# QKV in blocks of 512, 512, 512 and 384 columns, with transposed x, the weights and silu's halves at other residues of 256 bytes

## The chip, the core and the metric

The kernel runs on one core of a Trainium2 chip. The metric is device time in microseconds (us) of one execution; lower is better. A profile is taken of one further execution. TensorE (PE in the profile) multiplies, VectorE is DVE, ScalarE is ACT, GpSimd is POOL and SyncE is SP; PEld are TensorE's weight loads.

## What is computed

The reference normalises each of 2048 rows of x (640 columns), runs local attention over the result (32 heads of 20, each position looks at 8 positions in steps of 2 backwards), and gates the attention's output with a feed-forward part:

```python
xn = _layernorm(x, axis=-1)
s = _A_ref(xn, A_wqkv, A_wo)          # q, k, v = xn @ wqkv; scores; softmax; values; @ wo
g = _silu(_B_ref(xn, B_w1, B_w2))     # silu(silu(xn @ w1) @ w2)
return x + s * g
```

wqkv is 640 x 1920, wo 640 x 640, w1 640 x 1536, w2 1536 x 640, all float32.

## The kernel before, in words

**Precision.** TensorE is fed `float32r` operands. Every operand is split in a high part, which is its rounded copy, and a low part, which is the rest: `TH`/`TL` for transposed x (and later transposed attention output), `SH`/`SL` for silu(x W1), and the two halves of a slot of the weight ring `WR`. A product is three matmuls: high x high, low x high, high x low. So each logical matmul is issued three times, each with its own load of a 128x128 stationary tile and its own stream of up to 512 columns.

**Tiling.** The 2048 rows are four groups of 512 rows (`groups`), each of four tiles (`T`) of 128 rows. D = 640 is five chunks (`DC`) of 128, F = 1536 twelve (`FC`).

**Stages of a group**, in TensorE's order. `qkv_phase`: four blocks (`NQ`) of eight heads; for each block, five chunks c, four tiles t, three matmuls (L622 to L624): the stationary operand is a 128x128 piece of transposed x, the moving operand 480 columns of wqkv, which are 160 of q, 160 of k and 160 of v, into one PSUM bank for each t. ScalarE then evacuates k and v (L430) and q (L433), DMAs shift some rows of k and v (`halo`), and VectorE does scores and values (L467 to L509) with much delay, into `O`. In group 0 the first block is written out by hand (`first_quarter`, matmuls on L569) so that it can start before all weights have come: it works tile by tile, in passes over the chunks. `wo_phase` for the group before (L656 and L658 with TH/TL as stationary operand): it needs `O` transposed, which `o_chunk` does in five pieces (L419) at fixed places in the QKV stage (`O_AT`), or, for the last group, in the feed-forward stage (`OL_AT`). `ffn_phase`: for each of twelve chunks f, fifteen matmuls of 512 columns (L773 to L775; weights stationary, transposed x moving), silu twice on ScalarE (L779, L780) into `SH[f % 2]` and a float32 copy, the low part on VectorE (L781), and, one chunk later, 24 matmuls with silu's halves as the stationary operand and w2 as the moving one, 384 columns (L656) and 256 columns (L658) in turn. `wo_last` ends the program.

**Weights.** A ring of seven slots of 2 x 640 columns holds the next units (`units`, `w_load`, `w_next`, `w_done`). On first use a unit's raw float32 columns come in by DMA on SP's queue (`raw_load`, L338), are split by ScalarE (L361) and VectorE or GpSimd (L364), and both halves are stored to DRAM (L370); later uses load both halves by one DMA of GpSimd's queue (L353). High half first, low half directly behind it: for a QKV unit at 480 columns = 1920 bytes, for the others at 640 columns = 2560 bytes.

**Order.** TensorE's order is the program's. The other engines' order is made by a planner (`Weave`): every operation has a duration by a cost formula (`mm`, `ac`, `dv`, `po`; 0.45 us for issuing a DMA), a priority and the tiles that it reads and writes, and the planner simulates the program and emits it in order of the simulated start. The queues then run in that order.

**Memory.** All tiles come from one pool, one after the other in the order of the `sb.tile` lines (L194 to L220). `TH` and `TL` are 10240 bytes a tile, a ring slot 5120, silu halves 2048, all multiples of 256 in one partition; `mask` is 128 bytes, the statistics `ST` 48 each, of which a tile takes 64. Before, `st1` stands between `sh1`, `sl1` and `sh0`, `sl0`.

Of the kernel before, what the change touches and what calls it, by code (L numbers as in the profile page):

```python
# [8 lines left out]
F32 = mybir.dt.float32  # L9
F32R = mybir.dt.float32r  # L10
AF = mybir.ActivationFunctionType
# [3 lines left out]
P = 128  # L15
S, D, F, H, DH = 2048, 640, 1536, 32, 20
W = 8
DC, FC = D // P, F // P
NQ = 4
HQ = H // NQ  # L20
CQ = HQ * DH
J = 8
T = 4
TOK = T * P
HALO = W - 1
SCALE = DH ** -0.5
# [22 lines left out]
def tsl(t):  # L49
    return slice(t * P, (t + 1) * P)  # L50
# [120 lines left out]
def local_attention_silu_ffn(ctx: ExitStack, tc: tile.TileContext, x, wqkv, wo, w1, w2, out):  # L171
    nc = tc.nc
    pool = lambda name, bufs, **kw: ctx.enter_context(tc.tile_pool(name=name, bufs=bufs, **kw))
    sb = pool("sb", 1)
# [16 lines left out]
    def tiles(name, n, shape, dtype=F32):  # L191
        return [sb.tile(shape, dtype, name=f"{name}{i}") for i in range(n)]
# [4 lines left out]
    ST = [sb.tile([P, 2, 6], F32, name="st0")]  # L197
    TH = tiles("th", 2, [P, DC, TOK], F32R)
    TL = tiles("tl", 2, [P, DC, TOK], F32R)
    WR = tiles("w", RING, [P, 2 * D], F32R)  # L200
    SH = [None, sb.tile([P, TOK], F32R, name="sh1")]
    SL = [None, sb.tile([P, TOK], F32R, name="sl1")]
    ST.append(sb.tile([P, 2, 6], F32, name="st1"))
    SH[0] = sb.tile([P, TOK], F32R, name="sh0")
    SL[0] = sb.tile([P, TOK], F32R, name="sl0")
    SD = sb.tile([P, 2, T], F32, name="sd")
    mask = sb.tile([P, T, W], F32, name="mask")
    M = tiles("m", 2, [P, T, HQ])
    Z = tiles("z", 2, [P, 2, T, HQ])
    KV = tiles("kv", NQ, [P, 2, HALO + T, CQ])  # L210
    Q = tiles("q", NQ, [P, T, CQ])
    O = sb.tile([P, T, D], F32, name="o")
    PR = sb.tile([P, 2, W, CQ], F32, name="pr")
    L = tiles("l", 2, [P, T, W, HQ])
    E = tiles("e", 2, [P, T, W, HQ])
# [8 lines left out]
    PRK = [("pr", k) for k in range(DC)]  # L224
# [16 lines left out]
    mm = lambda n: n / 2400 + 0.0155  # L241
# [57 lines left out]
    for u in units:  # L299
        n = seen[u] = seen.get(u, 0) + 1  # L300
# [4 lines left out]
    raws = {}  # L305

    def width(u):
        return 3 * CQ if u[0] == "q" else D

    def raw_load(k):  # L310


        if k >= len(fresh):
            return
        i = fresh[k]
        u = units[i]
        n = width(u)
        if k < DC:
            r, kr = PR.rearrange("p t w m -> p (t w m)")[:, k * n:(k + 1) * n], [PRK[k]]
        elif k < early:  # L320
            s = (k - DC) % 6
            r, kr = (RAW[s], [("raw", s)]) if s < 2 else (G[:, s - 2, :], [("g", s - 2, 0), ("g", s - 2, CA)])
            r = r[:, :n]
        else:
            s = k % 2
            r, kr = RAW[s][:, :n], [("raw", s)]
        raws[i] = r, kr
        if u[0] == "q":
            _, q, c = u
            src = wqkv[c * P:(c + 1) * P, :].rearrange("p (s m) -> p s m", s=3)[:, :, q * CQ:(q + 1) * CQ]  # L330
            dst = r.rearrange("p (s m) -> p s m", s=3)
        elif u[0] == "w1":
            src = w1.rearrange("(c p) f -> p c f", p=P)[:, :, u[1] * P:(u[1] + 1) * P]
            dst = r.rearrange("p (c f) -> p c f", c=DC)
        else:
            m = wo if u[0] == "wo" else w2
            src, dst = m[u[1] * P:(u[1] + 1) * P, :], r
        dma(lambda: nc.sync.dma_start(dst, src), [], kr, n * P * 4, 1 + k if k < 2 * DC else clock[0] + 5)  # L338
# [87 lines left out]


    def evac_qkv(g, q, t, ps, kp):
        kv, qq = KV[q], Q[q]
        act(2 * CQ, lambda: nc.scalar.activation(  # L430
            kv[:, :, HALO + t, :], ps[:, CQ:3 * CQ].rearrange("p (s m) -> p s m", s=2), AF.Copy),
            [kp], [("kv", q, t)], 0)
        act(CQ, lambda: nc.scalar.activation(qq[:, t, :], ps[:, :CQ], AF.Copy), [kp], [("q", q, t)], 0)  # L433

    def halo(g, q):
        h, par = groups[g]
# [23 lines left out]

    def scores(g, q):
        i = q % 2
        l, e, m, kv, qq = L[i], E[i], M[i], KV[q], Q[q]
        hk = halo_keys(q)
        pr = 100 + 10 * (NQ * g + q)
        for t in range(0, T, 2):
            dve(2560, lambda t=t: nc.vector.tensor_tensor(  # L467
                out=PR, in0=win(qq[:, t:t + 2, :], W, 0), in1=win(kv[:, 0, t:t + 2, :], W, CQ), op=OP.mult),
                hk + [("q", q, t), ("q", q, t + 1)], PRK, pr, lock=True)
# [12 lines left out]
        act(256, lambda: nc.scalar.activation(e, l, AF.Exp, scale=SCALE), kl, [("e", i)], 0.5, "exp")  # L482
# [33 lines left out]
    def first_quarter(i):  # L516

        ps, ws = {}, []
# [41 lines left out]
        def products(t, steps):  # L560

            o, kp = ps[t]
            for k, c in steps:
                x, kx = (TL, "tl") if k == 1 else (TH, "th")
                wh, wl, kh, kl = ws[c]
                w, kw = (wl, kl) if k == 2 else (wh, kh)
                first, last = t not in given, given.get(t, 0) == 3 * DC - 1
                given[t] = given.get(t, 0) + 1
                pe(mm(480), lambda x=x, c=c, w=w, first=first, last=last: nc.tensor.matmul(  # L569
                    o[:, :3 * CQ], x[i][:, c, tsl(t)], w, start=first, stop=last), [(kx, i, c, t), kw], [kp])  # L570

        def passes(*ks):
            return [(k, c) for k in ks for c in range(DC)]
# [14 lines left out]
        for t in range(T):  # L588
            b, kp = bank()
# [18 lines left out]
    def qkv_phase(g, i, io):  # L608
        for q in range(NQ):
            if g == 0 and q == 0:  # L610
                ps = first_quarter(i)
            else:
                ps = [bank() for t in range(T)]
                for c in range(DC):
                    wh, wl, kh, kl = w_next("q", q, c)
                    for t in range(T):
                        o, kp = ps[t]

                        def unit(c=c, t=t, o=o, wh=wh, wl=wl):
                            o = o[:, :3 * CQ]  # L620
                            hi, lo = TH[i][:, c, tsl(t)], TL[i][:, c, tsl(t)]
                            nc.tensor.matmul(o, hi, wh, start=c == 0, stop=False)  # L622
                            nc.tensor.matmul(o, lo, wh, start=False, stop=False)  # L623
                            nc.tensor.matmul(o, hi, wl, start=False, stop=c == DC - 1)  # L624
# [231 lines left out]
```

## Time and profile before

| What | Value |
|---|---|
| median of 3 runs | 643.29 us (643.25 to 643.55) |
| the profiled execution | 643.21 us |
| its span, from the first instruction to the last | 641.4 us |
| granted TensorE clock | 1.000 |
| TensorE busy | 635.5 us, 99% of the span, 3497 matmuls |
| VectorE busy | 536.6 us, 84% |
| DMA | 162.44 MB, mean 253 GB/s |

A row of the groups reads: line, engine, operation, written tile <- read tiles, shapes, count | busy time, mean time of one in ns | idle time of the engine before them and what ended it. A row of the timeline reads: start in us, duration, engine, line, operation, tiles, shapes and count. A row of the waits reads: engine, tile, line <- whom it waited for: us in all, times, the longest. Matmuls are pipelined, and the profile models their ends, so that durations overlap; the distance from start to start is the time that they take. SPq rows are DMAs being issued by SyncE.

### The profile page before, as it was taken

The page shows a single profiled execution, that of the slowest core. Times are in us where ns is not written, and L with a number is a line of the kernel's source. Part 1 is how long each engine was busy: PE and PEld are TensorE (multiplying, and loading weights), DVE is VectorE, ACT ScalarE, POOL GpSimd, SP SyncE. Part 2 cuts the span into 40 slices and gives each one's busy share as a digit, 9 for nine tenths or more (in the row PEclk, how much of TensorE's full clock was granted, in tenths as well). Part 3 has the DMA queues.
Part 4 walks back from the last instruction along what each step waited for, and adds up shares of the span by engine and source line. Part 5 has one row for each costly group of instructions (what it writes and reads, how often), then busy time and mean ns, then how long its engine had stood idle before and what let it go on. Part 6 is the DMA issues. An engine that isn't in the chain of part 4 may idle for free.

```text
span 641.4 us, 9021 instructions
## 1 busy us (share of the span) xinstructions
PE 635.5 (99%) x3497; PEld 574.4 (90%) x3497; DVE 536.6 (84%) x539; ACT 207.1 (32%) x401; POOL 111.0 (17%) x168
## 2 busy tenths in 40 slices
PE   8999999999999999999999999999999999999997
PEld 6888899998889999999888999999988899899997
DVE  6699999999999889999849999998106999999714
ACT  5436453443534022324332112233313222223130
POOL 4500000001000331111211134111111113311100
PEclk9999999999999999999999999999999999999999
DMA  8999999776999997656699989765579997876522
GB/s 266 348 319 338 350 385 360 278 227 227 306 317 320 294 296 246 193 167 222 174 271 265 298 233 312 245 188 162 173 207 264 274 296 231 281 261 199 170 83 82
DMA packets 64938, 162.44 MB, mean 253 GB/s; under 512 B 5648, under 2 KB 28656, under 8 KB 64896
## 3 DMA queue, kind: packets, MB, share of 16 engines
q0 software_dynamic: 20016, 82.58, 42.5%
q1 hardware_dynamic: 44880, 79.29, 39.1%
q8 instruction: 27, 0.44, 0.3%
q14 instruction: 15, 0.12, 0.1%
HBM read 109.55 MB, written 34.16 MB: 224 GB/s over the span
## 4 chain that ended last, share of the span: by engine, by line
PE 98%; DMA 1%; SPq 1%; ACT 0%; DVE 0%; issue 0%
PE acc L656 22%; PE acc L658 15%; PE acc L623 10%; PE acc L624 10%; PE acc L622 10%; PE rot L775 9%; PE rot L773 9%; PE rot L774 9%; PE rot L419 2%; PE acc L569 2%; DMA pr<-in_A_wqkv_dram 1%; SPq L338 0%; PE rot L745 0%; PE rot L548 0%; SPq L578 0%; ACT w L361 0%
## 5 line engine op out<-in xcount | busy, mean ns | idle before, releaser
L656 PE MATMUL acc<-w,sh 128*128 128x384 f32 x384 | 114.8, 337 | 0.0
L623 PE MATMUL acc<-w,tl 128*128 128x480 f32 x300 | 114.6, 382 | 0.0
L622 PE MATMUL acc<-w,th 128*128 128x480 f32 x300 | 114.5, 382 | 0.0
L624 PE MATMUL acc<-w,th 128*128 128x480 f32 x300 | 113.3, 378 | 0.0
L658 PE MATMUL acc<-w,sh 128*128 128x256 f32 x384 | 107.2, 279 | 0.0
L467 DVE TENSOR_TENSOR pr<-q,kv 128x2560 f32<-128x2560 f32 x32 | 90.3, 2821 | 9.8 <-DMA kv<-kv 9.4
L773 PE MATMUL rot<-th,w 128*128 128x512 f32 x240 | 94.9, 396 | 0.0
L775 PE MATMUL rot<-th,w 128*128 128x512 f32 x240 | 93.7, 391 | 0.0
L774 PE MATMUL rot<-tl,w 128*128 128x512 f32 x240 | 93.7, 390 | 0.0
L499 DVE TENSOR_TENSOR pr<-e,kv 128x2560 f32<-128x2560 f32 x32 | 90.3, 2820 | 0.7
L470 DVE TENSOR_REDUCE l<-pr 128x128 f32<-128x2560 f32 x32 | 90.0, 2812 | 0.2
L779 ACT ACTIVATE sh<-rot 128x512 fp32r<-128x512 f32 x48 | 28.8, 599 | 160.3 <-PE rot L775 160.1
L504 DVE TENSOR_TENSOR pr<-pr 128x1280 f32<-128x1280 f32 x64 | 76.4, 1193 | 1.1
L658 PEld LDWEIGHTS acc<-w,sh 128*128 128x128 f32 x384 | 72.2, 188 | 1.5
L656 PEld LDWEIGHTS acc<-w,sh 128*128 128x128 f32 x384 | 72.1, 188 | 1.5
L353 POOL DMA_DIRECT2D w<-half_w x72 | 38.4, 533 | 189.0 <-PE acc L658 95.6
L353 POOL DMA_DIRECT2D w<-half_q x52 | 27.8, 534 | 243.5 <-PE rot L775 125.8
L622 PEld LDWEIGHTS acc<-w,th 128*128 128x128 f32 x300 | 56.3, 188 | 9.1
L624 PEld LDWEIGHTS acc<-w,th 128*128 128x128 f32 x300 | 56.3, 188 | 8.2
L623 PEld LDWEIGHTS acc<-w,tl 128*128 128x128 f32 x300 | 56.4, 188 | 7.9
L656 PE MATMUL acc<-w,sl 128*128 128x384 f32 x192 | 58.5, 336 | 0.0
L775 PEld LDWEIGHTS rot<-th,w 128*128 128x128 f32 x240 | 45.0, 188 | 9.7
(88 smaller groups left out, 977.6 us busy)
## 6 DMA issues: line engine op xcount, KB each, us to landing
w<-half_w POOLq DMA_DIRECT2D x72, 640.0 KB, 5.4
w<-half_q POOLq DMA_DIRECT2D x52, 480.0 KB, 4.3
half_w<-w SPq DMA_DIRECT2D x24, 640.0 KB
half_q<-w SPq DMA_DIRECT2D x20, 480.0 KB
w<-half_wo POOLq DMA_DIRECT2D x15, 640.0 KB, 5.3
kv<-kv SPq DMA_DIRECT2D x16, 560.0 KB
kv<-kv SPq DMA_DIRECT2D x16, 420.0 KB
gate<-in_B_w_dram SPq DMA_DIRECT2D x16, 320.0 KB
```

The costliest lines, as they stand in the source:

```text
L467: dve(2560, lambda t=t: nc.vector.tensor_tensor(out=PR, in0=win(qq[:, t:t + 2, :], W, 0), in1=win(kv[:, 0, t:t + 2, :], W, CQ), op=OP.mult ...
L470: dve(2560, lambda t=t: nc.vector.tensor_reduce(out=l[:, t:t + 2].rearrange("p t w h -> p (t w h)"), in_=PR.rearrange("p t w (h d) -> p (t ...
L499: dve(2560, lambda t=t, v=v: nc.vector.tensor_tensor(out=PR.rearrange("p t w (h d) -> p t (w h) d", d=DH), in0=e[:, t:t + 2].rearrange("p ...
L504: dve(2 * n * CQ, lambda n=n: nc.vector.tensor_tensor(out=PR[:, :, 0:n, :], in0=PR[:, :, 0:n, :], in1=PR[:, :, n:2 * n, :], op=OP.add), [] ...
L622: nc.tensor.matmul(o, hi, wh, start=c == 0, stop=False)
L623: nc.tensor.matmul(o, lo, wh, start=False, stop=False)
L624: nc.tensor.matmul(o, hi, wl, start=False, stop=c == DC - 1)
L656: nc.tensor.matmul(a[t][0][:, :CA], st, w[:, :CA], start=first, stop=last)
L658: nc.tensor.matmul(b[t // 2][0][:, h * CB:(h + 1) * CB], st, w[:, CA:], start=first and h == 0, stop=last, skip_group_check=True)
L773: nc.tensor.matmul(h, wh[:, cs], TH[i][:, c, :], start=c == 0, stop=False)
L774: nc.tensor.matmul(h, wh[:, cs], TL[i][:, c, :], start=False, stop=False)
L775: nc.tensor.matmul(h, wl[:, cs], TH[i][:, c, :], start=False, stop=c == DC - 1)
```

## The change

q's columns are cut differently from k's and v's. A block still brings the 160 columns of k and 160 of v of its eight heads, but with them 192 columns of q (`BQ`), so that three blocks have 512 columns and the last, with 64 of q, has 384. `Q` becomes one tile of 640 columns for each t; the scores of block q wait for the evacuations of blocks q - 1 and q. A raw QKV unit is loaded by two DMAs, q apart from k and v, and the planner is told 0.9 us for issuing them. The low half of a QKV unit begins 512 or 384 columns behind the high one, 2048 or 1536 bytes, both multiples of 256.

`mask` moves from behind the silu halves to before the weight ring, and `st1` to behind the ring and before all four silu halves. Modulo 256, `TH` and `TL` then begin at 0 (counted from the first of them), the weights at 128, the silu halves at 192; before, `TH`, `TL`, the weights, `sh1` and `sl1` began at 0 and `sh0` and `sl0` at 64.

```diff
+BQ = 192
...
     TL = tiles("tl", 2, [P, DC, TOK], F32R)
+    mask = sb.tile([P, T, W], F32, name="mask")
     WR = tiles("w", RING, [P, 2 * D], F32R)
-    SH = [None, sb.tile([P, TOK], F32R, name="sh1")]
-    SL = [None, sb.tile([P, TOK], F32R, name="sl1")]
     ST.append(sb.tile([P, 2, 6], F32, name="st1"))
-    SH[0] = sb.tile([P, TOK], F32R, name="sh0")
-    SL[0] = sb.tile([P, TOK], F32R, name="sl0")
+    SH = tiles("sh", 2, [P, TOK], F32R)
+    SL = tiles("sl", 2, [P, TOK], F32R)
     SD = sb.tile([P, 2, T], F32, name="sd")
-    mask = sb.tile([P, T, W], F32, name="mask")
...
-    Q = tiles("q", NQ, [P, T, CQ])
+    Q = sb.tile([P, T, D], F32, name="q")
...
     def width(u):
-        return 3 * CQ if u[0] == "q" else D
+        return qcols(u[1]) + 2 * CQ if u[0] == "q" else D
+
+    def qcols(b):
+        return min(BQ, D - b * BQ)
...
-            src = wqkv[c * P:(c + 1) * P, :].rearrange("p (s m) -> p s m", s=3)[:, :, q * CQ:(q + 1) * CQ]
-            dst = r.rearrange("p (s m) -> p s m", s=3)
+            w = qcols(q)
+            all3 = wqkv[c * P:(c + 1) * P, :].rearrange("p (s m) -> p s m", s=3)
+
+            def go():
+                nc.sync.dma_start(r[:, :w], all3[:, 0, q * BQ:q * BQ + w])
+                nc.sync.dma_start(r[:, w:].rearrange("p (s m) -> p s m", s=2), all3[:, 1:, q * CQ:(q + 1) * CQ])
+            dma(go, [], kr, n * P * 4, 1 + k if k < 2 * DC else clock[0] + 5, dur=0.9)
+            return
...
-        act(CQ, lambda: nc.scalar.activation(qq[:, t, :], ps[:, :CQ], AF.Copy), [kp], [("q", q, t)], 0)
+        act(w, lambda: nc.scalar.activation(Q[:, t, q * BQ:q * BQ + w], ps[:, :w], AF.Copy), [kp], [("q", q, t)], 0)
...
-                hk + [("q", q, t), ("q", q, t + 1)], PRK, pr, lock=True)
+                hk + [("q", b, u) for b in range(max(q - 1, 0), q + 1) for u in (t, t + 1)], PRK, pr, lock=True)
...
-                        pe(3 * mm(480), unit, t_keys(i, [c], [t]) + [kh, kl], [kp])
+                        pe(3 * mm(n), unit, t_keys(i, [c], [t]) + [kh, kl], [kp])
```

More of the change, by code (lines that the diff above doesn't have):

```diff
@@ L428, in evac_qkv @@
     def evac_qkv(g, q, t, ps, kp):
-        kv, qq = KV[q], Q[q]
+        kv, w = KV[q], qcols(q)
         act(2 * CQ, lambda: nc.scalar.activation(
-            kv[:, :, HALO + t, :], ps[:, CQ:3 * CQ].rearrange("p (s m) -> p s m", s=2), AF.Copy),
+            kv[:, :, HALO + t, :], ps[:, w:w + 2 * CQ].rearrange("p (s m) -> p s m", s=2), AF.Copy),
             [kp], [("kv", q, t)], 0)
-        act(CQ, lambda: nc.scalar.activation(qq[:, t, :], ps[:, :CQ], AF.Copy), [kp], [("q", q, t)], 0)
+        act(w, lambda: nc.scalar.activation(Q[:, t, q * BQ:q * BQ + w], ps[:, :w], AF.Copy), [kp], [("q", q, t)], 0)
     def halo(g, q):
@@ L462, in scores @@
         i = q % 2
-        l, e, m, kv, qq = L[i], E[i], M[i], KV[q], Q[q]
+        l, e, m, kv, qq = L[i], E[i], M[i], KV[q], Q[:, :, q * CQ:(q + 1) * CQ]
         hk = halo_keys(q)
@@ L568, in products @@
                 given[t] = given.get(t, 0) + 1
-                pe(mm(480), lambda x=x, c=c, w=w, first=first, last=last: nc.tensor.matmul(
-                    o[:, :3 * CQ], x[i][:, c, tsl(t)], w, start=first, stop=last), [(kx, i, c, t), kw], [kp])
+                pe(mm(512), lambda x=x, c=c, w=w, first=first, last=last: nc.tensor.matmul(
+                    o, x[i][:, c, tsl(t)], w, start=first, stop=last), [(kx, i, c, t), kw], [kp])
         def passes(*ks):
@@ L615, in qkv_phase, with unit @@
                     wh, wl, kh, kl = w_next("q", q, c)
+                    n = width(("q", q, c))
                     for t in range(T):
                         o, kp = ps[t]
-                        def unit(c=c, t=t, o=o, wh=wh, wl=wl):
-                            o = o[:, :3 * CQ]
+                        def unit(c=c, t=t, o=o, wh=wh, wl=wl, n=n):
+                            o = o[:, :n]
                             hi, lo = TH[i][:, c, tsl(t)], TL[i][:, c, tsl(t)]
```

## The prediction

> **What bounds the kernel now.** I read the page first, then the waits and the chain, then the timeline of TensorE stretch by stretch. The page gives the frame: the span, the busy row of TensorE, the chain by engine, and the costliest groups.
>
> ```profile
> span 641.4 us, 9021 instructions
> PE 635.5 (99%) x3497; PEld 574.4 (90%) x3497; DVE 536.6 (84%) x539; ACT 207.1 (32%) x401; POOL 111.0 (17%) x168
> PE 98%; DMA 1%; SPq 1%; ACT 0%; DVE 0%; issue 0%
> ```
>
> TensorE carries 98% of the chain. The waits say the same from the other side; the longest in which TensorE or its weight loads stood idle:
>
> ```profile
> PE rot L522 <- POOL ident masks.py:199: 1.4, 1, 1.4
> PEld acc L569 <- ACT w L361: 1.3, 3, 0.5
> PEld acc L569 <- DVE tl L556: 0.9, 1, 0.9
> PEld acc L658 <- ACT q L433: 0.8, 3, 0.3
> ```
>
> Apart from the first 25 us nothing is waited for, so the time is the number of matmuls times the distance from one start to the next. Durations on the page overlap (337 ns for a matmul that is followed 0.17 us later), so I use starts from the timeline, as pace = (last start - first start) / matmuls between. QKV in group 0, blocks 1 to 3, is 3 x 5 x 4 x 3 = 180 matmuls from the first row to the second; x W1 of chunk 3 is 15 from the third to the fourth; wo after group 0 has 60 pairs of 384 and 256 columns, and from its third pair, the fifth row, to the sixth are 58:
>
> ```profile
> 24.29 0.38 PE L622 MATMUL acc<-w,th 128*128 128x480 f32 x1
> 63.29 0.39 PE L773 MATMUL rot<-th,w 128*128 128x512 f32 x1
> 80.54 0.39 PE L773 MATMUL rot<-th,w 128*128 128x512 f32 x1
> 83.94 0.34 PE L656 MATMUL acc<-w,sh 128*128 128x384 f32 x1
> 203.41 0.34 PE L656 MATMUL acc<-w,tl 128*128 128x384 f32 x1
> 220.43 0.39 PE L773 MATMUL rot<-th,w 128*128 128x512 f32 x1
> ```
>
> 480 columns: 39.00 / 180 = 216.7 ns. 512 columns: 3.40 / 15 = 226.7 ns. A pair 384 + 256: 17.02 / 58 = 293.4 ns. With pace = a + b x columns, 226.7 = a + 512b and 293.4 = 2a + 640b give b = 0.417 ns and a = 13.3 ns. On that line 480 columns should take 213.3 ns; QKV takes 3.4 ns more for each matmul. So a fixed price stands on every matmul, and it is not the same everywhere. That is what the change can touch.
>
> **Part 1, the widths.** QKV is 4 groups x 4 blocks x 5 x 4 x 3 = 960 matmuls before and after, of the same 1920 columns in all. Before: 960 x 216.7 = 208.0 us. After: 720 of 512 columns and 240 of 384; on the line 720 x 226.7 + 240 x 173.3 = 163.2 + 41.6 = 204.8 us. Saved: **3.2 us**. All of it lies on TensorE, so on the path. Bounds: nothing, if the 3.4 ns belong to QKV and not to 480 columns; and 3.2, since the line is the cheapest that whole stretches show.
>
> **Part 2, silu's halves.** Worked out from the sizes of the tiles in the order of allocation (48 bytes of statistics take 64): before, transposed x, weights and the halves of odd chunks begin at the same residue modulo 256, the halves of even chunks 64 further. In h W2 the weights stream and a silu half is loaded meanwhile, so the trace has both distances. Chunk 1 (distance 0) runs from the first row to the second, x W1 behind it to the third, chunk 2 (distance 64) to the fourth, x W1 behind it to the fifth:
>
> ```profile
> 77.02 0.33 PE L656 MATMUL acc<-w,sh 128*128 128x384 f32 x1
> ...
> 87.40 0.40 PE L773 MATMUL rot<-th,w 128*128 128x512 f32 x1
> 90.84 0.33 PE L656 MATMUL acc<-w,sh 128*128 128x384 f32 x1
> ```
>
> (80.54 and 83.94 stand above.) The 24 matmuls of h W2 take 3.52 us at distance 0 and 3.46 us at 64, so the distance counts: 2.5 ns a matmul. But the 15 of x W1 that follow take 3.40 and then 3.44 us: two thirds of it is given back. After the change all chunks have distance 64 (192 - 128): 24 odd chunks gain 0.06 and lose 0.04, **0.5 us** in all; bounds 0 and 24 x 0.06 = 1.4 us.
>
> **Part 3, transposed x against the weights.** After the change they lie 128 apart: in QKV and wo, x is loaded (0) while weights stream (128); in x W1 the other way round. Nothing in x W1 or wo shows 128 now. But the low half of a QKV weight begins 480 x 4 = 1920 = 7.5 x 256 bytes after the high half, so L624, and the passes of block 0 that multiply by low halves, do stream at 128 from x. The groups of QKV from 25 to 63 us:
>
> ```profile
> L623 PE MATMUL acc<-w,tl 128*128 128x480 f32 x59 | 22.6, 382 | 0.0
> L624 PE MATMUL acc<-w,th 128*128 128x480 f32 x59 | 22.3, 377 | 0.0
> L622 PE MATMUL acc<-w,th 128*128 128x480 f32 x59 | 22.2, 377 | 0.0
> ```
>
> L624 is 2.5 ns below the mean of the two others. Block 0 has the same in pure runs, on the timeline:
>
> ```profile
> 20.17 0.82 PE L569 MATMUL acc<-w,th 128*128 128x480 f32 x3
> 21.05 0.60 PE L569 MATMUL acc<-w,th 128*128 128x480 f32 x2
> 22.14 1.25 PE L569 MATMUL acc<-w,tl 128*128 128x480 f32 x5
> 23.23 1.23 PE L569 MATMUL acc<-w,th 128*128 128x480 f32 x5
> ```
>
> The last five are x's high part times low halves, 128 apart: (24.29 - 23.23) / 5 = 212 ns, against 218 ns for the five at distance 0 before them. But the four from 20.17 to 21.05 are low halves of the tile before, 128 apart as well, and take 0.88 / 4 = 220 ns. So 128 gave 212 once and 220 once: 1.3 ns below or 6.7 above the line's 213.3, and 6 ns below or 2 above the 218 next to it. I take half of the 2.5 ns of L624, because the two runs have opposite signs, on the matmuls where the same roles hold: (960 + 480) x 1.25 = **1.8 us** saved. For the 720 of x W1, where the roles are swapped, I take nothing, the middle. Bounds: 6 ns to either side on all 960 + 480 + 720 = 2160 matmuls, 13 us down or up.
>
> A rule of the Trainium skill speaks against parts 2 and 3: TensorE: Matmul & The Clock Gate, Step-by-step, has two independent read ports, so that "Loading the next tile's weights doesn't steal SBUF read bandwidth from the running matmul." By it no residue could matter, parts 2 and 3 would be nothing, and the estimate would be 2.3 us higher. The trace disagrees at one place, the 3.52 against 3.46 us.
>
> **Part 4, the start.** Before 25 us TensorE does wait, for weights and x. The queue and the waits of VectorE:
>
> ```profile
> 3.05 2.55 SPq L338 DMA_DIRECT2D pr<-in_A_wqkv_dram  x4
> 6.30 0.61 SPq L390 DMA_DIRECT2D xin<-in_A_x_dram  x1
> 9.22 0.60 ACT L361 ACTIVATE w<-pr 128x480 fp32r<-128x480 f32 x1
> 9.99 0.61 ACT L361 ACTIVATE w<-pr 128x480 fp32r<-128x480 f32 x1 [0.17 <-DMA pr<-in_A_wqkv_dram]
> 11.70 0.49 DVE L534 BATCH_NORM_STATS2 st<-xin 128x6 f32<-128x320 f32 x1 [0.30 <-DMA xin<-in_A_x_dram]
> 12.25 0.89 DVE L556 TENSOR_TENSOR tl<-rot,th 128x384 fp32r<-128x384 f32 x2
> ```
>
> Weights arrive every 0.77 us (9.22 to 9.99) and are issued every 0.65 us (2.55 / 4). Each is now 512 / 480 as large, and issued as two DMAs, the second with 256 of the former 384 pieces: about 0.9 us between 0.65 and twice that. Then the issue sets the pace: 5 x (0.9 - 0.77) = 0.65 us later. The x tile that is issued at 6.30 is moved past by five extra issues, some 1.2 us; L534 waits for it already (0.30), and behind it on VectorE stands L556, the low part of tile 1, for which TensorE waited 0.9. If the order holds, that is up to 1.2 us more; the planner is told 0.9 us for an issue and may put L556 first. I take **1.0 us** lost; bounds 0.3 (only the bytes: 5 x 0.77 x 0.067) and 2.5. The other 15 double issues come in blocks 1 to 3 of group 0, when TensorE waits for nothing and weights lie up to seven units ahead in the ring, which hides them; cover gone, 0.25 us each. On SP's queue they pass the shifts of kv, for which the first product of the scores waits:
>
> ```profile
> L467 DVE TENSOR_TENSOR pr<-q,kv 128x2560 f32<-128x2560 f32 x32 | 90.3, 2821 | 9.8 <-DMA kv<-kv 9.4
> ```
>
> That delays VectorE by 0.25 us an issue at most, and not TensorE as long as VectorE has the slack shown next.
>
> **Edits at nothing.** Evacuation of q takes 192 columns instead of 160, and 64 in the last block:
>
> ```profile
> L430 ACT ACTIVATE kv<-acc 128x320 f32<-128x320 f32 x64 | 28.1, 439 | 47.2 <-PE acc L624 43.5 <-PE acc L569 2.7
> L433 ACT ACTIVATE q<-acc 128x160 f32<-128x160 f32 x64 | 19.3, 301 | 0.0
> ```
>
> 32 columns more are (439 - 301) / 160 x 32 = 28 ns, 48 times, beside an ACT that is 32% busy; cover gone, 1.3 us. Scores wait for two blocks of q, of which the earlier was evacuated a block before; written over, q is free before kv of the same block, which needs the later values pass. VectorE, 84% busy, is the cover of all gains: its last values pass before the fourth transpose of o in group 3 ends 605.57, the transpose starts 612.04:
>
> ```profile
> 605.08 0.49 DVE L507 TENSOR_TENSOR o<-pr 128x320 f32<-128x320 f32 x1
> 612.04 0.60 PE L419 MATMUL rot<-ident,o 128*128 128x128 f32 x4
> ```
>
> 6.5 us can be gained there before VectorE is late next; a gain of 5 us over four groups stays inside.
>
> **The sum.** The profiled execution took 643.21 us, its span 641.4 and 1.8 around it; the median of the runs is 643.29, the same within 0.1. 643.2 - 3.2 - 0.5 - 1.8 + 1.0 = **638.7 us**.
>
> **The rivals.** *Nothing but the count matters*: the fixed price is per matmul and belongs to the stage; QKV keeps its 216.7 on average, and residues do nothing. For it: the count and the columns are unchanged. Against: 3.52 and 3.46. It gives 643.2 + 1.0 = 644.2 us. The Trainium skill, same page, Back-to-back issue gap, has a warm matmul at columns / 2.4 plus a constant; by it QKV takes the same however it is cut into blocks, and the trace's 3.4 ns of 480 over the line speak against it. *128 is the bad distance*: load and stream meet more often at half a period than at none, in QKV, wo and x W1. For it: the 220 ns of the first low-half run. Against: L624 and the 212. Gains without part 3 are 3.2 + 0.5 - 1.0 = 2.7 us, so it decides from 2.7 / 2160 = 1.25 ns a matmul; at half of 6 ns, 3 x 2160 = 6.5 us, it gives 643.2 - 2.7 + 6.5 = 647.0 us; at all of it 653.5. *128 is the good distance everywhere*: 6 ns off each of 2160, 13 us, so 643.2 - 2.7 - 13 = 627.5 us. That is some 4 us a group, still inside VectorE's 6.5. For it: the 212 ns. Against: x W1's swapped roles stand in no row.
>
> **How the numbers follow.** Forecast 0.48, with a range of its own from 635 to 642.5 (part 1 missing or part 3 at its 2.5 ns, the start at 0.3 or 2.5); count only 0.17; bad distance 0.20; good distance 0.15. From 630 to 648 leaves out most of the good distance and the dearer half of the bad one, some 0.18. A measurement can tell 0.2%, 1.3 us, from no change. Faster: 0.9 of the forecast and all of the good distance, 0.43 + 0.15 = 0.58. Same: the rest of the forecast, most of count only and a little of the bad one, 0.19. Slower: 0.23.
>
> **What would show it.** Blocks 1 to 3 of group 0, now two of 512 columns and one of 384, should take 120 x 226.7 + 60 x 173.3 = 37.6 us on the line, where 39.00 stood, and 37.4 with part 3. x W1 at 226.7 a matmul means that swapped roles do nothing; 232 or more, the bad distance; 221 or less, the good one. The chunks of h W2 should all take 3.46. The first L622 should start at 24.29 + 1.0 for the start + 60 x 10 ns for block 0's width = 25.9. I am wrong if wo's pairs and x W1 leave 293.4 and 226.7 by more than 3 ns a matmul, or if VectorE appears as a releaser of L419.

## The result and the profile after

| | before | after |
|---|---|---|
| median of 4 runs | 643.42 us (643.25 to 643.72) | 650.84 us (650.71 to 651.26) |
| span of the profiled execution | 641.4 us | 648.9 us |
| granted TensorE clock | 1.000 | 1.000 |

The ratio is 1.0118, 95% interval 1.0105 to 1.013: the changed kernel is slower, by 7.4 us, where 4.6 us faster was forecast; 648 was the end of the range.

The page of after: the span, the busy row and the chain by engine.

```profile
span 648.9 us, 9080 instructions
PE 641.6 (99%) x3497; PEld 574.0 (88%) x3497; DVE 539.0 (83%) x539; ACT 207.4 (32%) x401; POOL 117.0 (18%) x168
PE 97%; SPq 1%; DMA 1%; DVE 1%; issue 0%
```

TensorE has the same 3497 matmuls and is as busy as before. The longest waits of its weight loads in after:

```profile
PEld acc L577 <- ACT w L369: 2.2, 3, 0.8
PEld rot L530 <- POOL ident masks.py:199: 1.4, 1, 1.4
PEld acc L577 <- DVE tl L564: 0.9, 1, 0.9
PEld acc L577 <- ACT th L560: 0.8, 2, 0.5
```

L577 is block 0, in the first 26 us; only there did the waits grow (for the weights from 1.3 to 2.2 us). The wait for q's evacuation after that is 0.8 us, as before. VectorE does not stand here as a releaser of L427, the transpose of o. So the time went into the distances from one matmul to the next. The timeline of TensorE in after (L631 is QKV, L782 the first matmul of an x W1, L665 the 384 columns of h W2 and wo); rows 1 and 2 bound blocks 1 to 3 of group 0, rows 3 to 5 a chunk of group 0, rows 6 to 8 wo after group 0 with its 60 pairs (its first pair, its second, and the x W1 behind it), rows 9 to 11 a chunk of group 1:

```profile
25.81 0.39 PE L631 MATMUL acc<-w,th 128*128 128x512 f32 x1
64.22 0.39 PE L782 MATMUL rot<-th,w 128*128 128x512 f32 x1
74.63 0.39 PE L782 MATMUL rot<-th,w 128*128 128x512 f32 x1
78.12 0.34 PE L665 MATMUL acc<-w,sh 128*128 128x384 f32 x1
81.57 0.39 PE L782 MATMUL rot<-th,w 128*128 128x512 f32 x1
...
204.85 0.34 PE L665 MATMUL acc<-w,th 128*128 128x384 f32 x1
...
205.35 0.34 PE L665 MATMUL acc<-w,th 128*128 128x384 f32 x1
...
222.27 0.39 PE L782 MATMUL rot<-th,w 128*128 128x512 f32 x1
...
232.83 0.39 PE L782 MATMUL rot<-th,w 128*128 128x512 f32 x1
236.31 0.34 PE L665 MATMUL acc<-w,sh 128*128 128x384 f32 x1
239.90 0.39 PE L782 MATMUL rot<-th,w 128*128 128x512 f32 x1
```

Blocks 1 to 3 take 64.22 - 25.81 = 38.41 us, where 39.00 stood and 37.6 was promised. x W1 takes 3.49 us a chunk, 232.7 ns a matmul, over the 232 that was to mean "bad distance". h W2, at the same distance of 64 in every chunk, takes 78.12 to 81.57 = 3.45 us in group 0 and 236.31 to 239.90 = 3.59 in group 1. wo's pairs are the one gain. Its 60 pairs take 222.27 - 204.85 = 17.42 us; the first holds a wait, and from the second on they take 16.92 / 59 = 286.8 ns, where 293.4 stood.

Adding up the distances between starts over the whole trace, by stage (us; a matmul's distance is counted to the stage in which it starts):

| stage (matmuls) | before | after | difference |
|---|---|---|---|
| start, up to the end of block 0 (105) | 22.91 | 24.43 | +1.5 |
| other QKV (900) | 196.47 | 197.04 | +0.6 |
| x W1 (720) | 165.57 | 168.34 | +2.8 |
| h W2 (1152) | 167.98 | 171.06 | +3.1 |
| wo (465) | 69.09 | 68.39 | -0.7 |

The transposes behind block 0 do not change, and the last 15 matmuls with the end of the kernel take 0.2 us more. With that the sum is +7.5 us, by which the span grew. Block 0 stands in the first row: its 60 matmuls are now 512 columns wide instead of 480, so that the 900 of the second row have 60 x 32 = 1920 columns fewer than before, 0.8 us at the prediction's 0.417 ns a column.

### The profile page after: what moved, and what is told of

Read it like the earlier page. It is cut to its first block, busy times and chain, and to the rows that moved or that the text cites. A ratio compares the mean times of both kernels' runs of the same rounds, so it can differ in the third digit from the quotient of the medians.

```text
span 648.9 us, 9080 instructions
## 1 busy us (share of the span) xinstructions
PE 641.6 (99%) x3497; PEld 574.0 (88%) x3497; DVE 539.0 (83%) x539; ACT 207.4 (32%) x401; POOL 117.0 (18%) x168
## 4 chain that ended last, share of the span: by engine, by line
PE 97%; SPq 1%; DMA 1%; DVE 1%; issue 0%
PE acc L665 22%; PE acc L667 15%; PE acc L633 10%; PE acc L632 10%; PE acc L631 10%; PE rot L783 9%; PE rot L782 9%; PE rot L784 9%; PE rot L427 2%; PE acc L577 1%; DMA xin<-in_A_x_dram 1%; SPq L336 0%; SPq L337 0%; PE rot L754 0%; DVE st L542 0%; PE rot L556 0%
## 5 line engine op out<-in xcount | busy, mean ns | idle before, releaser
L665 PE MATMUL acc<-w,sh 128*128 128x384 f32 x384 | 116.7, 341 | 0.0
L631 PE MATMUL acc<-w,th 128*128 128x512 f32 (+1 forms) x300 | 115.0, 383 | 0.0
L633 PE MATMUL acc<-w,th 128*128 128x512 f32 (+1 forms) x300 | 113.9, 380 | 0.0
L632 PE MATMUL acc<-w,tl 128*128 128x512 f32 (+1 forms) x300 | 113.8, 379 | 0.0
L782 PE MATMUL rot<-th,w 128*128 128x512 f32 x240 | 95.8, 399 | 0.0
L665 PEld LDWEIGHTS acc<-w,sh 128*128 128x128 f32 x384 | 72.0, 187 | 1.8
L631 PEld LDWEIGHTS acc<-w,th 128*128 128x128 f32 x300 | 56.4, 188 | 9.5
L665 PE MATMUL acc<-w,sl 128*128 128x384 f32 x192 | 59.5, 340 | 0.0
L790 DVE TENSOR_TENSOR sl<-sf,sh 128x512 fp32r<-128x512 f32 x48 | 41.5, 869 | 17.4 <-ACT sf L789 17.1
```

Of the source, the lines that this page charges most:

```text
L665: nc.tensor.matmul(a[t][0][:, :CA], st, w[:, :CA], start=first, stop=last)
L782: nc.tensor.matmul(h, wh[:, cs], TH[i][:, c, :], start=c == 0, stop=False)
```

## The experiments

The theory after the result: x and weights 128 apart are dear, and what the widths gain is eaten by that. The rival: the widths are dear (two DMAs a unit, other order, scores that wait for two blocks), and the residues do little. In every table below the times by stage are sums of distances between starts, as above.

**The layout alone.** Before's blocks of 480 columns, with the changed order of the tiles.

```diff
+    mask = sb.tile([P, T, W], F32, name="mask")
     WR = tiles("w", RING, [P, 2 * D], F32R)
-    SH = [None, sb.tile([P, TOK], F32R, name="sh1")]
...
     ST.append(sb.tile([P, 2, 6], F32, name="st1"))
+    SH = tiles("sh", 2, [P, TOK], F32R)
```

> The tiles moved as in the change, QKV left at 480 columns with one DMA a unit. Theory A (residues set the pace, 128 between x and weights is the bad distance): x W1 goes from 230.0 to 233.8 ns a matmul as in the changed kernel, h W2 from 167.98 to about 171 us, so 643.4 + 2.8 + 3.1 = about 649 us. Theory B (the width of QKV's blocks or its double DMAs are to blame, and x W1 and h W2 only follow the state that QKV leaves behind): within 1 us of 643.4.

647.69 us, ratio 1.0067 (1.0052 to 1.0082), against 643.29 for before. Two chunks of its timeline, the first in group 1, the second in group 3 (L771 is x W1, L654 h W2):

```profile
231.79 0.39 PE L771 MATMUL rot<-th,w 128*128 128x512 f32 x1
235.27 0.34 PE L654 MATMUL acc<-w,sh 128*128 128x384 f32 x1
238.87 0.39 PE L771 MATMUL rot<-th,w 128*128 128x512 f32 x1
...
548.29 0.39 PE L771 MATMUL rot<-th,w 128*128 128x512 f32 x1
551.78 0.34 PE L654 MATMUL acc<-w,sh 128*128 128x384 f32 x1
555.23 0.39 PE L771 MATMUL rot<-th,w 128*128 128x512 f32 x1
```

x W1 at 3.48 and 3.49, and h W2 at 3.60 in the one and 3.45 in the other: after's two faults are there without the widths. By stage: x W1 +2.8, h W2 +2.7, wo -0.75, QKV -0.65. That QKV gains a little here matters later: at 480 columns, and in this sequence, a distance of 128 was no worse than 0.

**The widths alone.** After's blocks, with before's order of the tiles.

```diff
+    WR = tiles("w", RING, [P, 2 * D], F32R)
+    SH = [None, sb.tile([P, TOK], F32R, name="sh1")]
...
     mask = sb.tile([P, T, W], F32, name="mask")
-    WR = tiles("w", RING, [P, 2 * D], F32R)
-    ST.append(sb.tile([P, 2, 6], F32, name="st1"))
-    SH = tiles("sh", 2, [P, TOK], F32R)
```

> QKV in blocks of 512, 512, 512 and 384 columns, every tile where it was before. Theory A: x W1 and h W2 as before (165.6 and 168.0 us), QKV and the first block at 226.7 ns for 512 columns, 3.2 us saved, 0.9 us lost at the start: 641.1 us. Theory B: 512 columns take 232 ns here too, QKV saves nothing: 644 us or more.

642.07 us, ratio 0.9983 (0.9973 to 0.9992). QKV falls from 196.47 to 193.42, by 3.05 us; the start costs 1.3. The rest that it loses is h W2 +0.5, nearly all of it one chunk in group 2 that waited for silu's low half from VectorE, and 0.2 each in wo and at the end. The rival is refuted: the widths gain, and the layout is what makes after slow.

**Only the weights back.** After with `mask` behind the silu halves again. x, weights and halves lie at 0, 0 and 64, so that halves and weights are 64 apart as in after, and x and weights 0 instead of 128.

```diff
-    mask = sb.tile([P, T, W], F32, name="mask")
     WR = tiles("w", RING, [P, 2 * D], F32R)
     ST.append(sb.tile([P, 2, 6], F32, name="st1"))
     SH = tiles("sh", 2, [P, TOK], F32R)
     SL = tiles("sl", 2, [P, TOK], F32R)
     SD = sb.tile([P, 2, T], F32, name="sd")
+    mask = sb.tile([P, T, W], F32, name="mask")
```

> As width_only, with all four silu halves 64 from the weights (x and weights still at distance 0). Theory A with part 2 of the prediction: 0.5 us below width_only, 640.6 us. If instead the pace of h W2 depends on the state that the stage before leaves, as the changed kernel's 3.45 us in group 0 and 3.59 us in group 1 hint, it can be off by 24 x 0.1 = 2.4 us to either side.

641.29 us, ratio 0.9976 (0.9967 to 0.9986): 9.5 us under after for one line, and the fastest kernel of this study. Its timeline: blocks 1 to 3 of group 0, and a chunk of group 1.

```profile
25.34 0.39 PE L631 MATMUL acc<-w,th 128*128 128x512 f32 x1
...
62.97 0.39 PE L782 MATMUL rot<-th,w 128*128 128x512 f32 x1
...
236.52 0.40 PE L782 MATMUL rot<-th,w 128*128 128x512 f32 x1
239.96 0.34 PE L665 MATMUL acc<-w,sh 128*128 128x384 f32 x1
243.42 0.40 PE L782 MATMUL rot<-th,w 128*128 128x512 f32 x1
```

62.97 - 25.34 = 37.63 us, where the line of columns gave 37.6 for these blocks. x W1 takes 3.44 and h W2 3.46. Against after: QKV 3.6 us less, x W1 2.3, h W2 4.1, wo 0.9 more, the start 0.5 less. Weights and halves both moved by 128, so that h W2's own distance is the same 64 in the two kernels; what differs is the stages ahead of it. So h W2 pays for their distance.

**The pace by itself.** Matmuls alone, 36 in a row of 512 columns or 18 pairs of 384 and 256, the loaded tile moved by 32 bytes from run to run. It leaves out all of the reference's computation.

```diff
+    # 512 d128
+    for k in range(36): nc.tensor.matmul(ps[5][:, :512], S[:, 32:160], M[:, 0:512], start=k == 0, stop=k == 35)
...
+    # pair d128
+    for k in range(18):
+        nc.tensor.matmul(ps[4][:, :384], S[:, 32:160], M[:, 0:384], start=k == 0, stop=k == 17)
+        nc.tensor.matmul(ps[5][:, :256], S[:, 32:160], M[:, 384:640], start=k == 0, stop=k == 17)
```

> No part of the reference is computed: matmuls of fixed operands alone, 36 of 512 columns (or 18 pairs of 384 and 256, or 36 of 480) for each distance of the loaded tile from the streamed one, 0 to 224 bytes in steps of 32, once directly behind one another and once each behind four transposes, the distances then in falling order. Theory A: the pace of 512 columns is 226.7 ns at distance 0 and about 232 at 128 and the same behind transposes. Rival: the pace is the same at all distances, and the differences in the kernel come from what runs beside it on other engines. Third: the same distance gives two paces, depending on what ran before.

This kernel, and the second one of matmuls alone below, ran once each; the granted clock was 1.00 in every stretch in which the paces were read. The timeline, a row for each run of 512 columns: L39 has the distance 0, L41 32, L47 128, L49 160, L51 192, L53 224; then the first rows of the pairs, L87 at 0, L91 at 32, L95 at 64, L99 at 96, L103 at 128, L107 at 160:

```profile
17.05 8.33 PE L39 MATMUL acc<-mov,stat 128*128 128x512 f32 x36
25.22 8.55 PE L41 MATMUL acc<-mov,stat 128*128 128x512 f32 x36
...
50.44 8.53 PE L47 MATMUL acc<-mov,stat 128*128 128x512 f32 x36
58.81 8.55 PE L49 MATMUL acc<-mov,stat 128*128 128x512 f32 x36
67.20 8.40 PE L51 MATMUL acc<-mov,stat 128*128 128x512 f32 x36
75.44 8.56 PE L53 MATMUL acc<-mov,stat 128*128 128x512 f32 x36
...
179.58 0.33 PE L87 MATMUL acc<-mov,stat 128*128 128x384 f32 x1
184.86 0.34 PE L91 MATMUL acc<-mov,stat 128*128 128x384 f32 x1
190.14 0.34 PE L95 MATMUL acc<-mov,stat 128*128 128x384 f32 x1
195.52 0.34 PE L99 MATMUL acc<-mov,stat 128*128 128x384 f32 x1
200.80 0.34 PE L103 MATMUL acc<-mov,stat 128*128 128x384 f32 x1
205.97 0.33 PE L107 MATMUL acc<-mov,stat 128*128 128x384 f32 x1
```

Start to start, by 36: 226.9 ns at 0, 232.5 at 128, 233.1 at 160, 228.9 at 192. So at 512 columns 0 is the cheapest of all and 128 costs 5.6 ns. This is theory A; the rival, that other engines make the difference, is refuted, since none works beside these runs or those of the pairs. Pairs, by 18: 293.3 at 0, 298.9 at 64, 287.2 at 128. In long runs pairs and full width thus want opposite distances.

wo after groups 0 to 2 is such a long run of pairs, and in after it has the pace of these pairs, 286.8 ns; but the last wo of after, at the same distance 128, ran at 181 + 119 ns a pair and lost 0.3 us. A further run of 512 columns with both operands moved by 128 came back to 226.7 from its tenth matmul on (227.9 over all 36): there the distance counts, not the place. That the period is 256 bytes is not shown: every distance that is called 0 here is also a multiple of 512. The runs of 480 columns, from their second matmul on, took 216.4 ns at 0, 216.2 at 64 and 217.8 at 128.

But 298.9 for pairs at 64 does not fit before and the kernel above, which have 24 such matmuls in 3.45 us, 288 ns a pair.

**Halves at 128.** By the long runs, h W2 should be cheapest there. First with after's widths and the weights at 0 (the diff is against the kernel with only the weights back), then with before's widths.

```diff
-    ST.append(sb.tile([P, 2, 6], F32, name="st1"))
+    mask = sb.tile([P, T, W], F32, name="mask")
     SH = tiles("sh", 2, [P, TOK], F32R)
     SL = tiles("sl", 2, [P, TOK], F32R)
+    ST.append(sb.tile([P, 2, 6], F32, name="st1"))
     SD = sb.tile([P, 2, T], F32, name="sd")
-    mask = sb.tile([P, T, W], F32, name="mask")
```

> The widths of the change, x and weights at distance 0 as before, silu's halves 128 from the weights. By the table of paces that was measured with the matmuls alone, a pair of 384 and 256 columns takes 286.6 ns at distance 128 and 293.4 at 0: h W2 takes 576 x 286.6 = 165.1 us instead of 168.5 of width_only, and the kernel 642.1 - 3.4 = 638.7 us. Rival (the pace in the kernel depends on what ran before, and the table does not carry over): within 1 us of width_sh64's 641.3.

> The kernel before with nothing changed but silu's halves 128 from the weights. By the table h W2 takes 165.1 instead of 168.0 us: 643.3 - 2.9 = 640.4 us. Rival: x W1 behind it loses as much, as behind distance 64 (3.44 instead of 3.40 us), and 24 x 0.04 = 1.0 us is given back: 641.4.

643.09 us, ratio 0.9999 (0.9989 to 1.0008), and 644.18, ratio 1.0012 (1.0003 to 1.0021). Both forecasts missed, and so did their rivals, 641.3 and 641.4. A chunk of the first of them:

```profile
73.51 0.40 PE L782 MATMUL rot<-th,w 128*128 128x512 f32 x1
76.98 0.35 PE L665 MATMUL acc<-w,sh 128*128 128x384 f32 x1
80.46 0.40 PE L782 MATMUL rot<-th,w 128*128 128x512 f32 x1
```

h W2 takes 3.48 and not the 12 x 287.2 = 3.45 of the long run, and x W1 behind it 3.47 instead of 3.40. The starts show why: in h W2 they are 184, 120, 178, 118, 174, 116, 175 and 120 ns apart before they settle at 168 and 118, and in x W1 241, 237, 234, 236, 224, 231, 236, 228, 233 and 231 before 227. That adds up to 0.04 and 0.06 us a chunk, about the two differences. Runs of 24 and 15 matmuls are short against the eight to ten that a changed distance takes to settle. In the profiled execution of the first kernel two chunks of h W2 also waited for silu's low half from VectorE, 0.8 us together.

**Weights at 64, halves at 192**, so that x W1 has the distance 64 and h W2 128 (the diff is against the same kernel).

```diff
-    WR = tiles("w", RING, [P, 2 * D], F32R)
     ST.append(sb.tile([P, 2, 6], F32, name="st1"))
+    WR = tiles("w", RING, [P, 2 * D], F32R)
+    mask = sb.tile([P, T, W], F32, name="mask")
     SH = tiles("sh", 2, [P, TOK], F32R)
...
-    mask = sb.tile([P, T, W], F32, name="mask")
```

> As width_sh128 with the weights 64 from x and the halves 128 from the weights. By the table x W1 (stream x, load weights 64 further) takes 233.2 ns instead of 226.7, 720 x 6.5 = 4.7 us more; QKV of 512 columns (stream weights, load x 64 before, which is 192) takes 228.9, 720 x 2.2 = 1.6 us more; h W2 stays at 286.6 for a pair and wo at 293.4: about 645 us if width_sh128 takes 638.7. Rival (only 128 between x and weights is bad): as width_sh128.

648.73 us, ratio 1.0088 (1.0071 to 1.0104). x W1 took 3.50 us a chunk, 15 times the 233.3 ns of the long run at that distance. h W2 took 3.59 in most chunks, at the very distance at which it took 3.48 in the run above. The rival, that only 128 between x and weights is bad, is refuted. The forecast was 6.3 us over the kernel with halves at 128, and 5.6 came, but that is luck: x W1 lost 2.0 us where 4.7 were forecast, QKV 0.6 where 1.6 were, and h W2 2.3 where nothing was.

**Sequences.** What is left is that one distance has two paces. Matmuls alone again, 15 of 512 columns and 12 pairs in turn, at the distances of five layouts; no other engine works beside them until 249 us, when VectorE begins to copy results out. All of the reference's computation is left out.

```diff
+    for k in range(15): nc.tensor.matmul(ps[0][:, :512], S[:, 32:160], M[:, 0:512], start=k == 0, stop=k == 14)
+    for k in range(12):
+        nc.tensor.matmul(ps[2][:, :384], S[:, 48:176], M[:, 32:416], start=k == 0, stop=k == 11)
+        nc.tensor.matmul(ps[3][:, :256], S[:, 48:176], M[:, 416:672], start=k == 0, stop=k == 11)
```

> Matmuls alone; the kernel leaves out all of the reference's computation. In turn 15 matmuls of 512 columns and 12 pairs of 384 and 256 as in the feed-forward stage, six chunks each, at the distances of five layouts: before's even chunks (0, then 64), before's odd chunks (0, then 0), after (128, then 64), halves at 128 (0, then 128), weights at 64 (64, then 128); and after's with four transposes ahead of each h W2. Theory (the pace of a short run depends on the one before it too): h W2 at 64 takes 3.44 to 3.46 us a chunk behind x W1 at 0 and 3.58 to 3.60 behind x W1 at 128, and with transposes between them 3.46; at 128 it takes 3.48, not the 12 x 286.6 = 3.44 of a long run, and x W1 behind it 3.47 instead of 3.40. Rival (the distance of the run itself decides, the rest of the kernel made the difference): h W2 at 64 takes 12 x 300 = 3.60 us in every sequence, at 0 12 x 293.4 = 3.52, at 128 3.44, and x W1 3.40 at 0 and 3.49 at 128 and 64.

The timeline, h W2 and the x W1 behind it in one chunk of each of four sequences: before's even chunks (L65, L68), after's (L139, L142), weights at 64 (L213, L216), and two of after's with four transposes between x W1 and h W2 (L237 to L250):

```profile
43.57 0.34 PE L65 MATMUL acc<-mov,stat 128*128 128x384 f32 x1
47.02 3.61 PE L68 MATMUL acc<-mov,stat 128*128 128x512 f32 x15
...
127.54 0.34 PE L139 MATMUL acc<-mov,stat 128*128 128x384 f32 x1
131.00 3.65 PE L142 MATMUL acc<-mov,stat 128*128 128x512 f32 x15
...
212.15 0.34 PE L213 MATMUL acc<-mov,stat 128*128 128x384 f32 x1
215.74 3.66 PE L216 MATMUL acc<-mov,stat 128*128 128x512 f32 x15
...
241.33 0.60 PE L237 MATMUL acc<-ident 128*128 128x128 f32 x4
245.35 3.64 PE L243 MATMUL acc<-mov,stat 128*128 128x512 f32 x15
248.82 0.60 PE L244 MATMUL acc<-ident 128*128 128x128 f32 x4
252.70 3.65 PE L250 MATMUL acc<-mov,stat 128*128 128x512 f32 x15
```

Behind x W1, h W2 at 64 takes 3.45 and 3.46 us, at 128 behind an x W1 at 64 it takes 3.59. With transposes, the same h W2 of after and its transposes take 4.02 us once and 3.88 the next time. Matmuls alone thus repeat the kernels' x W1 and h W2 in these five layouts, but for the 3.59 of after's groups 1 to 3, which came here only with the transposes.

The rival, that a run's own distance decides, is refuted (it had 3.60 at 64, and 3.44 at 128). The theory held in that what comes before decides, but it had 3.59 for after's sequence and 3.46 with transposes, and the sequences showed mostly the reverse. The starts show two patterns of pairs at 64 that each keep themselves up: 171 and 116 ns, and 182 and 118. All six chunks of after's sequence fell into the first, and three of the four with transposes into the second; two of these three ran before VectorE did anything, so no other engine is needed for the two paces. What turned the fourth back is not shown: a copy by VectorE began at 249.03 us, just ahead of it.

After itself has both patterns behind the same x W1. In group 0, from 78.12 us, the starts of h W2 are 177, 118, 175 and 116 ns apart and then 171 and 116; in group 1, from 236.31 us, 177 and 118 and then 182 and 118. So the pattern stood after the first few matmuls, and it stayed for the rest of the stage in these runs. Group 0 mostly fell into the first, and groups 1 to 3 mostly into the second, which is also the 298.9 ns of the long run at 64. Why the groups differ is not shown; the stage ahead of x W1 is QKV in group 0 and wo in the others, but the layout alone had mostly the second pattern in group 0 and mostly the first in group 3.

**The start.** Before with two DMAs for a raw QKV unit:

```diff
-            src = wqkv[c * P:(c + 1) * P, :].rearrange("p (s m) -> p s m", s=3)[:, :, q * CQ:(q + 1) * CQ]
...
+            def go():
+                nc.sync.dma_start(r[:, :CQ], all3[:, 0, q * CQ:(q + 1) * CQ])
+                nc.sync.dma_start(r[:, CQ:].rearrange("p (s m) -> p s m", s=2), all3[:, 1:, q * CQ:(q + 1) * CQ])
```

> The kernel before, QKV's blocks still of 480 columns, with each raw QKV unit loaded by two DMAs and the planner told 0.9 us, as in the change. The prediction's part 4 without the larger units: 0.4 to 1.2 us lost before 25 us, so 643.7 to 644.5. Rival: the issue is hidden, 643.3.

644.40 us, ratio 1.002 (1.001 to 1.0029); the start is 0.5 us longer, about half of what the kernel lost (0.2 more lie at the end of its span, the rest outside it), and the wait of block 0 for its weights went from the 1.3 of before to 2.0:

```profile
PEld acc L574 <- ACT w L366: 2.0, 3, 1.0
```

Then the kernel of 641.29 us with a first block of 480 columns and one DMA. There are two versions; the second adds the wait in the last line of the diff, and its expectation says what the first lacked.

```diff
-BQ = 192
+QS = (0, 160, 352, 544, 640)
...
-        act(n, lambda: nc.scalar.activation(r[:, :n], raw, AF.Copy), kr, [kh], 1000 + due)
+        wider = u[0] == "q" and i >= RING and n > width(units[i - RING])
+        act(n, lambda: nc.scalar.activation(r[:, :n], raw, AF.Copy), kr, [kh, kl] if wider else [kh], 1000 + due)
```

> The kernel with blocks of 512, 512, 512 and 384 columns, weights at 0 and all silu halves at 64, with the blocks cut as 480, 512, 512 and 416 columns instead: 160, 192, 192 and 96 columns of q. Block 0 is loaded by one DMA a unit again, and the matmuls on the first block are as wide as before. Theory (the start lost 1.05 us there, of which the second DMA has about 0.5 and the width of the 60 matmuls of block 0 the other half): the start is back at 22.9 us, the 180 matmuls of 480 columns in groups 1 to 3 take 3.4 ns over the line each, 0.6 us more, and 240 at 416 against 384 and 512 columns leave the total of columns as it is. Net 0.4 us below 641.29: 640.9 us. Rival (the start is set by x and the order of the queues, not by block 0): 641.9.

> The kernel with blocks of 480, 512, 512 and 416 columns again, but a ring slot's new high half, where it is wider than the one it replaces, now waits for the readers of the old low half too. In the run before, the wider high half lay over the first 32 columns of the low half that the last five matmuls of block 0 still had to read, so that 98 rows of group 0 came out different, and TensorE waited for those writes twice, 0.31 and 0.33 us. Theory (block 0's width and its second DMA make the start dear, and those two waits are the error's alone): the start is 23.70 - 0.5 = 23.2 us and the QKV stage stays at the 195.1 us of the run before, since a 480 block puts its low half 128 from x and disturbs the 512 blocks behind it; 642.37 - 0.5 = 641.9 us. Rival (QKV's 195.1 came of the error too, and goes back to 193.4 + 0.6): 640.7.

642.37 us, ratio 0.999 (0.9981 to 0.9999), and 645.04, ratio 1.0036 (1.0023 to 1.0049). Both forecasts of the whole missed, and the parts can be read: the start came back to 22.76 us in the second, so block 0's width and second DMA are its price. But QKV rose to 195.1, 1.7 more than with blocks of 512 and 384, in both. The second expectation lays this to the 480 block disturbing the 512 blocks behind it, and that is not so: in the second kernel their 60 matmuls take 13.60 to 13.89 us, as in the kernel of 641.29 us. Of the 1.7 us, 0.8 are the 1920 columns that block 0 hands to the others; the rest lies in the blocks of 480 and 416 columns, which the other kernel does not have. In the second the new wait pushed ScalarE's work on silu behind it, once:

```profile
PEld acc L669 <- ACT sh L792: 2.7, 1, 2.7
```

## Why the prediction was wrong

**What bounds it** held: in after no wait is new beyond the start, VectorE was never late, and the whole difference beyond the start lies in distances between matmuls.

**Part 1, the widths**, held in kind, and the gain came a fifth smaller. Its 3.2 us are for all 960 matmuls, and the 60 of block 0 are 0.6 dearer in that sum; for the other 900 the same line gives 3.8 us, and 3.05 were measured with the widths alone. Blocks 1 to 3 of group 0 came as forecast, 37.63 us for 37.6 where x and weights lie at 0. The shortfall lies in groups 1 to 3, where transposes of o stand between the matmuls: 1.7 us were gained instead of 2.4. The long runs confirm that 480 columns lie over the line: 216.4 ns at 0, where the line has 213.3.

The rival that only the count matters fell with it. So did the Trainium skill's columns / 2.4 plus a constant (TensorE: Matmul & The Clock Gate, Back-to-back issue gap), which the page gives for an isolated matmul and by which the 960 would have taken the same: with the weights at 0 blocks of 512 and 384 columns took 226.7 and 173.8 ns a matmul in group 0 (13.60 and 10.43 us for 60), and 480 columns took 216.4 in the long run, which leaves 13.3, 13.8 and 16.4 ns over columns / 2.4 and no one constant.

**Part 4, the start**, held: with block 0's width it comes to 1.0 + 0.6 = 1.6 us, and 1.5 were measured in after, 1.3 with the widths alone and 1.05 with the weights at 0, of which two DMAs make 0.5. The first L631 starts at 25.81 us, where 25.9 was forecast.

**Part 3 is the step that failed.** It took half of the 2.5 ns of L624 as a gain at distance 128 on QKV and wo, and nothing for x W1: -1.8 us. Measured: QKV +3.6 (197.04 against 193.41, 4.0 ns a matmul), x W1 +2.8 (3.9 ns), wo -0.7 to -0.9. The row that it rested on does not show the distance. In the kernel with the layout alone, still at 480 columns, the first two matmuls of three (L620, L621) have the distance 128 and the third (L622), on the low half, has 0. Its groups from 25 to 63 us:

```profile
L621 PE MATMUL acc<-w,tl 128*128 128x480 f32 x60 | 22.7, 379 | 0.0
L620 PE MATMUL acc<-w,th 128*128 128x480 f32 x59 | 22.3, 378 | 0.0
L622 PE MATMUL acc<-w,th 128*128 128x480 f32 x59 | 22.1, 375 | 0.0
```

The third is 3.5 ns below the mean of the others at distance 0, as L624 was 2.5 below at 128. From start to start it is 3.3 ns below them in both kernels. So the third is short at either distance, and its gain can't be put down to 128; why it is short, no run shows. The long runs of 480 columns, 216.4 ns at 0 and 217.8 at 128, show no gain either, and the 0.65 us that the layout alone took off QKV show only that 128 did no harm there. Then the choice was carried to another width. The change made 720 of QKV's 960 matmuls 512 wide, and there the distance 128 costs 5.6 ns in a long run and as much in the kernel: blocks 1 and 2 of group 0 took 13.94 us each, against 13.60 with the weights at 0, 5.7 ns a matmul. Before's trace had no matmul of 512 columns at that distance, so its rows could not show this; the bounds of 13 us to both sides allowed for it, and the middle was a choice.

**Part 2 failed too, by a way that it did not list.** It said that all chunks of h W2 take 3.46 us since all lie at distance 64. At 0 for x and weights that is so, and all halves at 64 saved 1.0 us of x W1 and h W2 together (0.5 forecast; 0.2 of the 1.0 is a shorter wait for VectorE in one chunk). Behind an x W1 at 128, h W2 took 3.59 in most chunks of groups 1 to 3: 3.1 us more than before. The hint stood in the prediction: x W1 took 3.40 or 3.44 us by the distance of the stage ahead of it. I read it as a part of the gain given back, and not as a sign that a stage's pace depends on its predecessor.

**The sum**, with what the runs showed: start +1.5, QKV -3.05 by the widths and +3.6 by the distance, x W1 +2.8, h W2 +3.1, wo -0.7, the end +0.2: +7.5 us of span.

**The rivals.** "128 is the bad distance" was right in its sign and near in size (647.0 at half of its price, 653.5 at all), for QKV and x W1. It was wrong for wo after groups 0 to 2, whose pairs gained 6.6 ns, and did not have h W2. It had been given 0.20. Its opposite, 627.5, held for no stage but these.

**The rule of the Trainium skill** that loading does not steal read bandwidth from the running matmul (TensorE: Matmul & The Clock Gate, Step-by-step), from which the prediction drew that no residue could matter, does not save that conclusion: 226.9 and 232.5 ns for the same 36 matmuls with the loaded tile moved by 128 bytes. Whether the rule itself fails, by a conflict of reads, is not shown: no run looked at what the two reads do to each other, only at their distance. Why a distance has two paces stays open as well.

## What to carry to other kernels

Where every matmul loads its own stationary tile, the distance between loaded and streamed tile, here within 256 bytes, is a parameter worth several ns a matmul. It must be measured at the width that the kernel will have and in the sequence that it will run in: 128 did no harm at 480 columns and cost 5.6 ns at 512. A row that differs by a few ns from its neighbours shows a cause only when the cause is moved and the difference moves with it; here it stayed. Before moving tiles together with another change, run the move alone: here one line of allocation hid a gain of 2.0 us behind a loss of 9.5. A table of long runs does not carry over to stages of 15 and 24 matmuls, of which eight to ten are spent getting from one pattern to the next.

## What the runs showed of the hardware

- The pace of loaded matmuls in long runs (one execution), by distance of the two tiles in bytes: 512 columns 226.9 ns at 0, 228.9 at 192, 232.5 to 233.1 at 128 and 160; pairs of 384 and 256 columns 293.3 at 0, 298.9 at 64, 287.2 at 128.
- At one distance a run of pairs can go at two paces, and kept the one into which it fell: at 64 171 + 116 ns or 182 + 118, which is 3.45 or 3.59 us for 24 matmuls behind an x W1 at 128; at 128 3.48 or 3.59 us, and in long runs 168 + 118 (wo after groups 0 to 2 of after) or 181 + 119 (its last wo).
- A change of distance took up to ten matmuls to settle, with starts 224 to 241 ns apart where 227 follow.
- Four transposes between two stages can turn the pace of the second: after's h W2 went at 171 + 116 ns in six chunks of six without them, and at 182 + 118 in three of four with them.
